# A fused convolution and feed-forward kernel whose start-up is rearranged: first convolution over four quadrants, transposes inside unit 0, second convolution in two cuts

## The chip, the cores and the metric

The kernel runs on one core of a Trainium2 chip. The metric is the device time of one execution in microseconds (us). A profile of one execution gives, for each engine, when every instruction ran: TensorE (PE, with its weight loads as PEld), VectorE (DVE), ScalarE (ACT), GpSimd (POOL) and SyncE (SP). PE multiplies; DVE and ACT copy, scale and add; POOL and SP here mostly start DMA transfers.

## The reference

```python
def _attn_ref(x, weight):              # x (8, 4096, 192) f32, weight (8, 7)
    w = np.exp(weight - np.max(weight, axis=-1, keepdims=True))
    w = w / (np.sum(w, axis=-1, keepdims=True) + 1e-09)
    x_pad = np.concatenate([np.zeros((B, 6, D)), x], axis=1)
    idx = np.arange(S)[:, None] + np.arange(7)[None, :]
    x_unf = x_pad[:, idx, :].reshape(B, S, 7, H, D // H)
    return np.einsum('hk,bskhg->bshg', w, x_unf).reshape(B, S, D)

def _moe_ref(x, w_in, w_out):          # w_in (192, 2048), w_out (2048, 192)
    h = x @ w_in
    return np.maximum(0.01 * h, h) @ w_out
```

A causal convolution with seven taps along the sequence (the taps are a softmax, one set for each of eight heads of 24 channels), and then a two-layer network with a leaky ReLU between the layers, for 32768 tokens.

## The kernel before

The 192 channels are cut into three chunks of 64. The eight sequences are worked on in pairs: one sequence of a pair lies on partitions 0 to 63, the other on 64 to 127 (called `e` = 0 and 1). A block is 512 tokens of both sequences of a pair; there are 32 blocks. The first two blocks are cut in halves of 256 tokens, so the work runs over `groups`: four halves, then 30 whole blocks.

For a group, three things happen. The convolution makes `yt` from `xt` (x, transposed so that channels lie on partitions). `mm1` multiplies `yt` by `w_in` into a PSUM tile `ph` (128 x 1024 f32) and ACT turns `ph` into `g` with the leaky ReLU (L501); for a half group there are eight such units, called U0 to U7 here for the first group, and U8 and on for the second. Each unit of a half group is 12 matmuls of 256 columns: two slices `i` of the hidden layer, three chunks, two sequences, where the two sequences use different halves of PE's rows and run side by side, so a unit is six pairs. Two `ph` buffers take turns. The second layer multiplies `g` by `w_out` into PSUM (L511 for the four half groups, L574 later); its first three pairs run ahead of U8. DVE makes the convolution of the groups behind the second.

The change lies wholly in the start-up, up to the end of the first group. The order of each engine's instructions is the order in which the program issues them (a manual schedule); an engine waits on semaphores in that order. What is done there, with the lines of the profile:

- POOL starts the transfers of `w_in` (L314, in two column halves of 1024, each in two row parts), `x_rows` (L148: 256 tokens for the second group, then for the third) and `w_out` (L346), and later blocks of x (L152, L99).
- PE keeps itself busy with matmuls of ones (`warm`, L358), spreads the taps over the partitions (`select`, L394: the exponentials as a sum of three bf16 parts, hi, mid and a rest), and transposes the first group's x (L179); ACT copies it to `xt` (L199).
- For the convolution on PE, a tap is a 64 x 64 diagonal matrix, one for each of two bf16 parts (p = 0 is hi, 1 is mid), seven taps and three chunks: `diag[c][:, p, k]`. They are made from an identity `ident2` and the taps `whm` (f32): DVE makes five wide products (L413, seven taps at once, or four for chunk 1), ACT ten single ones (L421). A conv matmul (L257) is 64 x 64 with 256 columns and takes one quadrant of PE: row half by `e`, column half by where its result goes. With `cross` the result of one sequence goes to the other's partitions, so that four matmuls, two straight and two crossed, can run side by side. `run` zips the lists of two chunks, so one place of the order is two or four matmuls. The first convolution takes 28 places: seven of two (chunk 0, hi), seven of four (chunk 0, mid, and chunk 2, hi), seven of four (chunk 1, mid, and chunk 2, mid), seven of two (chunk 1, hi).
- The results are scaled by `rsum` (one over the softmax's sum) while ACT (L452) and DVE (L276, L271) copy them from PSUM to `yt`.
- `w_in` is wanted on both partition halves: `spread_down` (L320) and `spread_up` (L323) copy 64 partitions to the other 64 on DVE.
- PE then transposes the second group's x out of `x_rows[1]` (L188, 12 matmuls, `transpose_first(1)`), DVE copies the result to `xt` (L199), and U0 starts.
- The second group's chunk 1 is convolved on DVE (L226, L232); its chunks 0 and 2 on PE in 14 places of four matmuls, in cuts of 6, 5 and 3 places behind U1, U3 and U5 (`CUTS`). Behind U6, PE transposes the third group's x.

Of the kernel before, what the change touches and what calls it, by code (L numbers as in the profile page):

```python
# [10 lines left out]
FP32 = mybir.dt.float32  # L11
BF16 = mybir.dt.bfloat16
# [3 lines left out]
def kernel(  # L16
# [8 lines left out]
    nc = tc.nc  # L25

    B, S, D = x.shape
    H, K = weight.shape
# [7 lines left out]
    CH = 64  # L36
# [7 lines left out]
    NBLK = (B // 2) * NB  # L44
    NHALF = 2
    RUN = 4
    NPEC = 3
    FILL = 48
    VK = 4
    FIRST = (0, 2, 1)  # L50
    SKEW = [(c, k) for k in range(2) for c in range(2)]
    pair = iter([(0, 2), (1, 2), (0, 3), (1, 3), (0, 4), (1, 4), (0, 5)])
    for k in range(K):
        SKEW += [(2, k), next(pair)]
    SKEW += [(1, 5), (0, 6), (1, 6)]
    CUTS = {1: (0, 6), 3: (6, 11), 5: (11, 14)}
    GB = 32
    NR = D // (2 * GB)

# [135 lines left out]
    def evac_first(q, *copies):  # L195
        dst = xt[0][:, :, HALO + q * HT : HALO + (q + 1) * HT]
        dst = dst.rearrange("p c (s k) -> p s c k", s=HS)
        for s, t in enumerate(ptr.pop(q)):
            copies[s](out=dst[:, s], in_=t)  # L199
# [36 lines left out]
                )  # L236
        return jobs

    def pe_conv_jobs(grp, c, parts=(0, 1), cross=False, apart=False):

        blk, t0, T = grp
        accs = [
            psum_o.tile([128, ST], FP32, name=f"acc{i}", tag="po")
            for i in range(2 if apart else 1)
        ]
        jobs = []
        for p in parts:
            for k in range(K):  # L250
                a = BASE + k + blk * ST + t0
                both = []
                for e in range(2):
                    ps = slice(e * CH, (e + 1) * CH)
                    to = slice((e ^ cross) * CH, ((e ^ cross) + 1) * CH)
                    both.append(
                        lambda k=k, p=p, a=a, ps=ps, to=to, acc=accs[e * apart]: nc.tensor.matmul(  # L257
                            out=acc[to, :T], lhsT=diag[c][ps, p, k, :],
                            rhs=xt[0][ps, c, a : a + T],
                            start=(k == 0 and p == parts[0]),  # L260
                            stop=(k == K - 1 and p == parts[1]),
                        )
                    )
                jobs.append(both)

        def evac(*scale):
            if blk not in yt:
                yt[blk] = yt_pool.tile([128, NCH, ST], BF16, name="yt")
            y = yt[blk][:, c, t0 : t0 + T]
            if not cross:  # L270
                scale[0](y, accs[0][:, :T], rsum[:, c, :])  # L271
                return
            for e in range(2):
                ps = slice(e * CH, (e + 1) * CH)
                frm = slice((1 - e) * CH, (2 - e) * CH)
                scale[e](y[ps], accs[e * apart][frm, :T], rsum[frm, c, :])  # L276

        return jobs, evac

    def run(*lists):  # L280
        for slots in zip_longest(*lists, fillvalue=()):
            for both in slots:
                for job in both:
                    job()
# [31 lines left out]
            in_=moe_w_in[rows : rows + ps[1], n * WF : (n + 1) * WF],  # L316
        )

    def spread_down(n):
        nc.vector.tensor_copy(out=w_in[n][0:CH, 1, :], in_=w_in[n][CH:128, 0, :])  # L320

    def spread_up(n):
        nc.vector.tensor_copy(out=w_in[n][CH:128, 1:3, :], in_=w_in[n][0:CH, 0:3:2, :])  # L323

    def w_in_of(f, e, c, m0, m1):
        n, f = divmod(f, NFC // NPW)
# [29 lines left out]
    def warm(n, cols=HT):  # L356
        for _ in range(n):
            nc.tensor.matmul(  # L358
                out=wa[:, 0, 0:cols], lhsT=ones[:, 0:128], rhs=ones[:, 0:cols],
                start=True, stop=True,  # L360
            )
# [41 lines left out]
    cast_first(0, 0, nc.scalar.copy)  # L403
    cast_first(0, 1, nc.scalar.copy, slice(0, 1))
    cast_first(0, 1, nc.vector.tensor_copy, slice(1, 2))
    whm = const_pool.tile([128, NCH, 2, K + 1], FP32, name="whm")
    nc.vector.tensor_copy(out=whm, in_=wps_hm)


    diag = [const_pool.tile([128, 2, K, CH], BF16, name=f"diag{c}") for c in range(NPEC)]  # L410

    def diag_wide(c, p, n):
        nc.vector.tensor_mul(  # L413
            diag[c][:, p, 0:n],
            ident2[:, None, :].to_broadcast([128, n, CH]),
            whm[:, c, p, 0:n, None].to_broadcast([128, n, CH]),
        )

    def diag_each(c, p, ks):
        for k in ks:  # L420
            nc.scalar.activation(  # L421
                out=diag[c][:, p, k, :], in_=ident2,
                func=mybir.ActivationFunctionType.Copy, scale=whm[:, c, p, k : k + 1],
            )


    warm(1, 192)
    transpose_first(0, lambda: select(wps_l, slice(2, 3)))
    wps_l = wps_l[:, :, 0, 0]
    warm(1, ST)  # L430
    warm(1, 384)
    evac_first(0, nc.scalar.copy, nc.scalar.copy)
    for p in range(2):
        diag_wide(0, p, K)
    diag_wide(2, 0, K)
    diag_wide(1, 1, VK)
    diag_wide(2, 1, K)
    diag_each(1, 1, range(VK, K))
    diag_each(1, 0, range(K))
    wml = const_pool.tile([128, NCH, K + 1], FP32, name="wml")  # L440
    nc.vector.tensor_add(wml, wps_l, whm[:, :, 1])
    rsum = const_pool.tile([128, NCH, 1], FP32)
    nc.vector.scalar_tensor_tensor(
        out=rsum, in0=wml[:, :, K:], scalar=1e-9, in1=whm[:, :, 0, K:],
        op0=mybir.AluOpType.add, op1=mybir.AluOpType.add,
    )
    nc.vector.reciprocal(rsum, rsum)
    spread_down(0)
    spread_up(0)

    def act_scale(out, in_, scale):
        nc.scalar.activation(  # L452
            out=out, in_=in_, func=mybir.ActivationFunctionType.Copy, scale=scale
        )

    pe_0, evac_0 = pe_conv_jobs(groups[0], 0)
    pe_2, evac_2 = pe_conv_jobs(groups[0], 2, cross=True, apart=True)
    pe_1, evac_1 = pe_conv_jobs(groups[0], 1, (1, 0))
    run(pe_0[:K])
    run(pe_0[K:], pe_2[:K])  # L460
    evac_0(act_scale)
    run(pe_1[:K], pe_2[K:])
    run(pe_1[K:])
    evac_2(act_scale, nc.vector.tensor_scalar_mul)
    evac_1(act_scale)
    transpose_first(1)
    evac_first(1, nc.vector.tensor_copy, nc.vector.tensor_copy)
    wk = const_pool.tile([128, NCH, K], FP32, name="wk")
    nc.vector.tensor_add(wk, whm[:, :, 0, 0:K], wml[:, :, 0:K])
    nc.vector.tensor_mul(wk, wk, rsum.to_broadcast([128, NCH, K]))  # L470


    g, po, acc2, osb, seal = {}, {}, {}, {}, None
# [8 lines left out]
    def mm1(grp, u, M):  # L482
        blk, t0, T = grp
        y = yt[blk]
        nf = ST // T
        ph = psum_h.tile([128, 2, ST], FP32, name="ph", tag="ph")
        chunks = range(NCH) if blk or t0 else FIRST
        for n in range(nf * NCH):
            i, c = n // NCH, chunks[n % NCH]
            f = nf * u + i  # L490
            for e in range(2):
                ps = slice(e * CH, (e + 1) * CH)
                for m in range(0, 128, M):
                    nc.tensor.matmul(  # L494
                        out=ph[m : m + M, e, i * T : (i + 1) * T],
                        lhsT=w_in_of(f, e, c, m, m + M),
                        rhs=y[ps, c, t0 : t0 + T],
                        start=(c == chunks[0]),
                        stop=(c == chunks[-1]),
                    )  # L500
        act = nc.scalar.activation(  # L501
            out=g[blk][:, nf * u : nf * (u + 1), :, t0 : t0 + T],
            in_=ph.rearrange("p e (i t) -> p i e t", i=nf),
            func=mybir.ActivationFunctionType.Prelu, alpha=0.01,
        )
        return act
# [149 lines left out]
    for i, grp in enumerate(groups):  # L656
# [11 lines left out]
        for j in range(steps):  # L668
            early = between.get((i, j), (0, 0))
            for u in range(2 * j, 2 * j + 2):  # L670
                mm2_slots(i, early[u % 2])
                mm1(grp, u, 128 if i <= NSW else CH)
                if i == 0 and u == 0:
                    conv_1 = conv_jobs(groups[1], (1,))
                    for job in conv_1[:3]:
                        job()
                    spread_down(1)
                    spread_up(1)
                    for job in conv_1[3:]:
                        job()  # L680
                    pe_0, evac_0 = pe_conv_jobs(groups[1], 0)
                    pe_2, evac_2 = pe_conv_jobs(groups[1], 2, cross=True)
                if i == 0 and u in CUTS:
                    cut = slice(*CUTS[u])
                    run(pe_0[cut], pe_2[cut])
                if i == 0 and u == 5:
                    evac_0(nc.vector.tensor_scalar_mul)
                    evac_2(nc.vector.tensor_scalar_mul, nc.vector.tensor_scalar_mul)
                if i == 0 and u == 6:
                    transpose_first(2)  # L690
            jobs = ahead[per * j : per * (j + 1)]
            if T == ST:

# [3 lines left out]
                    job()  # L697
                jobs = []
            mm2_slots(i, quota[j] - sum(early))
            if i == 0 and j == 3:  # L700
                evac_first(2, nc.vector.tensor_copy, nc.vector.tensor_copy)
            if i == 1 and j == 1:
                load_x(3, transpose_x(2))
            for job in jobs:
# [47 lines left out]
```

## Time and profile before

| what | value |
|---|---|
| median of 4 runs | 681.21 us (681.05 to 681.47) |
| the profiled execution | 681.47 us |
| its span (first to last instruction) | 679.7 us |
| first matmul of U0 starts | 9.46 us |
| DVE busy / ACT busy | 481.2 / 518.7 us |
| granted PE clock from 3.5 us on | 1.0 |

The span is what the profile's instructions cover; the rest of the time lies around it. A timeline line has the start in us from the span's beginning, the time that the merged instructions cover, engine, line of the program and operation, tiles written and read, the shape, how many instructions were merged, and in brackets how long the engine was idle before and what released it. A busy engine is not always an engine that does new work: a matmul's record is longer (0.27 us for 256 columns) than the distance to the next one (0.11 us).

### The profile page before, as it was taken

Reading aid. Unit: us, or ns where it says so; the run is one execution under the profiler, and the core shown is the slowest. Engines: PE = TensorE matmul, PEld = TensorE weight load, DVE = VectorE, ACT = ScalarE, POOL = GpSimd, SP = SyncE. Lnnn points to the kernel's source line nnn. Section 1 sums busy time; section 2 is a strip of 40 time slices with the busy share of each in tenths; the row PEclk is TensorE's granted clock in tenths of the full one; section 3 lists DMA queues with packets and bytes.
Section 4 is the critical chain, followed back from the end, with each engine's and each line's share of the span. In section 5 each row is a group of like instructions: output and inputs, shape, how many; then the busy total and the mean of one; then the engine's idle time right before and its main releaser. Section 6 shows DMA issues by size and latency. Waiting matters only on the chain.

```text
span 679.7 us, 27093 instructions
## 1 busy us (share of the span) xinstructions
PE 675.4 (99%) x12444; PEld 446.8 (66%) x12444; DVE 481.2 (71%) x811; ACT 518.7 (76%) x608; POOL 146.7 (22%) x205
## 2 busy tenths in 40 slices
PE   9999999999999999999999999999999999999998
PEld 6997666666666666666666666666666666666667
DVE  7989468766768667778667687667786676876612
ACT  7899777777777778777777877777777777777781
POOL 7455210222201222102222012222022220000000
PEclk9999999999999999999999999999999999999999
DMA  9898846666647557456566476565565573321123
GB/s 153 96 106 111 57 78 89 80 63 74 90 77 96 71 55 89 80 87 87 63 66 92 76 95 76 56 85 83 84 87 67 62 96 72 72 56 33 34 49 94
DMA packets 213890, 53.27 MB, mean 78 GB/s; under 512 B 209296, under 2 KB 213392, under 8 KB 213776
## 3 DMA queue, kind: packets, MB, share of 16 engines
q0 software_dynamic: 98752, 13.97, 30.2%
q1 hardware_dynamic: 115008, 37.57, 27.7%
q8 instruction: 97, 1.59, 1.0%
q14 instruction: 17, 0.14, 0.1%
q10 hardware_dynamic: 16, 0.00, 0.0%
HBM read 28.31 MB, written 25.17 MB: 79 GB/s over the span
## 4 chain that ended last, share of the span: by engine, by line
PE 98%; DMA 1%; POOL 0%; issue 0%; DVE 0%; POOLq 0%
PE ph L494 49%; PE acc L574 44%; PE po L511 5%; DMA x_rows<-in_x_dram 1%; PE acc L257 0%; POOL w_in L314 0%; PE ptr L188 0%; POOL x_rows L148 0%; POOL sel L300 0%; DVE o_sb L624 0%; POOL ident masks.py:199 0%; POOL sel L298 0%; POOL ident masks.py:197 0%; POOLq masks.py:199 0%; POOLq L736 0%
## 5 line engine op out<-in xcount | busy, mean ns | idle before, releaser
L501 ACT ACTIVATE g<-ph 128x1024 bf16<-128x1024 f32 x512 | 496.6, 1021 | 140.7 <-PE ph L494 140.5
L232 DVE SCALAR_TENSOR_TENSOR yt<-xt,wk,yt 128x512 bf16<-128x512 bf16 (+1 forms) x582 | 381.2, 726 | 0.2
L494 PE MATMUL ph<-yt,w_in 64*64 64x512 bf16 (+2 forms) x6048 | 377.1, 369 | 0.0
L574 PE MATMUL acc<-g,w_out 64*64 64x512 bf16 x5568 | 339.9, 376 | 0.0
L494 PEld LDWEIGHTS <-w_in 64*64 64x64 bf16 (+1 forms) x6048 | 229.1, 131 | 103.1 <-issue 0.8
L574 PEld LDWEIGHTS <-w_out 64*64 64x64 bf16 x5568 | 178.6, 118 | 118.7
L99 POOL DMA_DIRECT2D x_bf<-in_x_dram x180 | 134.3, 777 | 410.4 <-DMA xt<-x_bf 408.6
L596 DVE STREAM_TRANSPOSE o_t<-acc 128x512 f32<-128x512 f32 x87 | 73.3, 883 | 181.5 <-PE acc L574 181.5
L511 PE MATMUL po<-w_out,g 64*128 64x192 bf16 (+1 forms) x640 | 36.8, 243 | 0.0
L511 PEld LDWEIGHTS <-g 64*128 64x128 bf16 (+1 forms) x640 | 32.5, 95 | 3.2 <-issue 0.4
L226 DVE TENSOR_SCALAR yt<-xt,wk 128x512 bf16<-128x512 bf16 (+1 forms) x97 | 29.1, 325 | 3.4 <-DMA xt<-x_bf 3.2
L584 ACT COPY junk<-junk 128x1 f32<-128x1 f32 x58 | 11.1, 192 | 4.1
L624 DVE COPY o_sb<-po 128x192 f32<-128x192 f32 x8 | 2.8, 357 | 6.8 <-PE po L511 3.8
L257 PE MATMUL acc<-xt,diag 64*64 64x256 bf16 x140 | 5.5, 272 | 0.2 <-ACT xt L199 0.2
L624 ACT COPY o_sb<-po 128x192 f32<-128x192 f32 x16 | 5.1, 324 | 0.3
L257 PEld LDWEIGHTS <-diag 64*64 64x64 bf16 x140 | 4.3, 106 | 1.3 <-DVE diag L413 0.6
L152 POOL DMA_DIRECT2D x_half<-in_x_dram x6 | 4.3, 726 | 1.1 <-DMA w_in<-in_moe_w_in_dram 0.9
L358 PE MATMUL warm<-const-bfloat16-1.0 128*128 128x512 bf16 (+3 forms) x12 | 3.7, 457 | 0.8 <-PEq L736 0.8
L358 PEld LDWEIGHTS <-const-bfloat16-1.0 128*128 128x128 bf16 x12 | 1.4, 127 | 2.5 <-issue 2.5
L148 POOL DMA_DIRECT2D x_rows<-in_x_dram x4 | 2.9, 741 | 0.0
L413 DVE TENSOR_TENSOR diag<-ident,whm 128x448 bf16<-128x448 bf16 (+1 forms) x5 | 2.6, 581 | 0.0
L421 ACT ACTIVATE diag<-ident,whm 128x64 bf16<-128x64 bf16 x10 | 2.5, 335 | 0.0
(47 smaller groups left out, 23.7 us busy)
## 6 DMA issues: line engine op xcount, KB each, us to landing
out_dram<-o_t SPq DMA_DIRECT2D x112, 192.0 KB, 4.6
x_bf<-in_x_dram POOLq DMA_DIRECT2D x180, 64.0 KB, 3.1
out_dram<-o_sb SPq DMA_DIRECT2D x8, 192.0 KB, 3.0
xt<-x_bf SPq DMA_TRANSPOSE x90, 3.7
w_out<-in_moe_w_out_dram POOLq DMA_DIRECT2D x2, 384.0 KB, 7.8
out_dram<-o_t SPq DMA_DIRECT2D x8, 96.0 KB, 2.3
out_dram<-o_sb SPq DMA_DIRECT2D x8, 96.0 KB, 1.7
w_in<-in_moe_w_in_dram POOLq DMA_DIRECT2D x2, 256.0 KB, 5.1
```

What stands on the lines that cost most here:

```text
L99: ins = nc.gpsimd.dma_start(out=t[:, c, :, e, :], in_=src[2 * rp + e, :, :, c * CH : (c + 1) * CH],)
L226: lambda s=src, d=dst, c=c: nc.vector.tensor_scalar_mul(d, s, wk[:, c, 0:1])
L232: lambda s=src, d=dst, c=c, k=k: nc.vector.scalar_tensor_tensor(out=d, in0=s, scalar=wk[:, c, k : k + 1], in1=d, op0=mybir.AluOpType.mult, ...
L257: lambda k=k, p=p, a=a, ps=ps, to=to, acc=accs[e * apart]: nc.tensor.matmul(out=acc[to, :T], lhsT=diag[c][ps, p, k, :], rhs=xt[0][ps, c, a ...
L358: nc.tensor.matmul(out=wa[:, 0, 0:cols], lhsT=ones[:, 0:128], rhs=ones[:, 0:cols], start=True, stop=True,)
L494: nc.tensor.matmul(out=ph[m : m + M, e, i * T : (i + 1) * T], lhsT=w_in_of(f, e, c, m, m + M), rhs=y[ps, c, t0 : t0 + T], start=(c == chun ...
L501: act = nc.scalar.activation(out=g[blk][:, nf * u : nf * (u + 1), :, t0 : t0 + T], in_=ph.rearrange("p e (i t) -> p i e t", i=nf), func=my ...
L511: return nc.tensor.matmul(out=po[m], lhsT=g[b][ps, fc, e, s * 128 : (s + 1) * 128], rhs=w_out[ps, fc, :], start=start, stop=stop,)
L574: ins = nc.tensor.matmul(out=acc2[gi, r][e * CH : (e + 1) * CH, 0:T], lhsT=w_out_of(ps, fc, r), rhs=g[b][ps, fc, e, t0 : t0 + T], start=fi ...
L584: seal = nc.scalar.copy(out=junk, in_=junk)
L596: nc.vector.transpose(out=osb[gi, 0][:, 0 : T // GB, :, r], in_=acc2.pop((gi, r))[:, 0:T].rearrange("p (j k) -> p j k", k=GB),)
L624: ins = copy(out=o_sb[:, n % 2, :], in_=po.pop(n))
```

## The change

In words, in the order of the program:

- Taps: `whm` (f32) becomes `taps` (bf16), each tap stored twice side by side. All six diagonals (three chunks, two parts) are made by DVE, by a product over pairs of neighbouring columns; ACT makes none.
- One more warm-up matmul of 192 columns stands ahead of the first convolution.
- First convolution in 21 places of four: chunk 0's hi taps go straight into one PSUM tile and its mid taps crossed into another at the same time; then chunks 1 and 2, hi then mid, at the same time. The two tiles of chunk 0 are joined: ACT scales the crossed one into an f32 tile `low`, and DVE computes `hi * rsum + low`. One half of chunk 2 uses a bank of the `wps` tile.
- `spread_up(0)` is split in two copies, one ahead of `spread_down(0)` and one behind the join; `wk` (f32 taps for DVE's convolution) is computed earlier.
- The transposes of `x_rows[1]` move from ahead of U0 to the inside of U0: U0 does chunk 0 for both slices, then the transposes run, then chunks 1 and 2. The DVE copies follow U0 in the program.
- Second convolution: cuts of 7 and 7 places behind U1 and U4, its evacuation behind U4's cut; the third group's transposes behind U5 and not U6, and the DVE copies of them directly after.

```diff
-    CUTS = {1: (0, 6), 3: (6, 11), 5: (11, 14)}
+    CUTS = {1: (0, K), 4: (K, 2 * K)}
...
+    def y_of(grp, c):
         blk, t0, T = grp
...
+        if blk not in yt:
+            yt[blk] = yt_pool.tile([128, NCH, ST], BF16, name="yt")
+        return yt[blk][:, c, t0 : t0 + T]
+
+    def acc_tile():
+        return psum_o.tile([128, ST], FP32, name="acc", tag="po")
...
-        def evac(*scale):
...
+        def evac(*scale, out=None):
+            out = y_of(grp, c) if out is None else out
             if not cross:
-                scale[0](y, accs[0][:, :T], rsum[:, c, :])
+                scale[0](out, accs[0][:, :T], rsum[:, c, :])
                 return
...
+    def spread_up(n, slots=slice(0, 3, 2), copy=nc.vector.tensor_copy):
+        to = slice(slots.start // 2 + 1, (slots.stop - 1) // 2 + 2)
+        copy(out=w_in[n][CH:128, to, :], in_=w_in[n][0:CH, slots, :])
...
-    whm = const_pool.tile([128, NCH, 2, K + 1], FP32, name="whm")
-    nc.vector.tensor_copy(out=whm, in_=wps_hm)
+    taps = const_pool.tile([128, NCH, 2, K + 1, 2], BF16, name="taps")
+    nc.vector.tensor_copy(
+        out=taps, in_=wps_hm[..., None].to_broadcast([128, NCH, 2, K + 1, 2])
+    )
...
+    def diag_wide(c, p):
+        shape = [128, K, CH // 2, 2]
         nc.vector.tensor_mul(
-            diag[c][:, p, 0:n],
-            ident2[:, None, :].to_broadcast([128, n, CH]),
-            whm[:, c, p, 0:n, None].to_broadcast([128, n, CH]),
-        )
+            diag[c][:, p].rearrange("p k (m t) -> p k m t", t=2),
+            ident2.rearrange("p (m t) -> p m t", t=2)[:, None].to_broadcast(shape),
+            taps[:, c, p, 0:K, None, :].to_broadcast(shape),
+        )
...
     warm(1, 384)
+    warm(1, 192)
     evac_first(0, nc.scalar.copy, nc.scalar.copy)
-    for p in range(2):
-        diag_wide(0, p, K)
-    diag_wide(2, 0, K)
-    diag_wide(1, 1, VK)
-    diag_wide(2, 1, K)
-    diag_each(1, 1, range(VK, K))
-    diag_each(1, 0, range(K))
...
+    diag_wide(0, 0)
+    diag_wide(0, 1)
+    diag_wide(1, 0)
+    nc.vector.tensor_add(wml, wps_l, taps[:, :, 1, :, 0])
+    diag_wide(2, 0)
...
+    diag_wide(1, 1)
     nc.vector.reciprocal(rsum, rsum)
+    diag_wide(2, 1)
+    spread_up(0, slice(0, 1))
     spread_down(0)
-    spread_up(0)
+    wk = const_pool.tile([128, NCH, K], FP32, name="wk")
+    nc.vector.tensor_add(wk, taps[:, :, 0, 0:K, 0], wml[:, :, 0:K])
+    nc.vector.tensor_mul(wk, wk, rsum.to_broadcast([128, NCH, K]))
...
-    pe_0, evac_0 = pe_conv_jobs(groups[0], 0)
-    pe_2, evac_2 = pe_conv_jobs(groups[0], 2, cross=True, apart=True)
-    pe_1, evac_1 = pe_conv_jobs(groups[0], 1, (1, 0))
-    run(pe_0[:K])
-    run(pe_0[K:], pe_2[:K])
-    evac_0(act_scale)
-    run(pe_1[:K], pe_2[K:])
-    run(pe_1[K:])
-    evac_2(act_scale, nc.vector.tensor_scalar_mul)
+    hi = acc_tile()
+    low = const_pool.tile([128, HT], FP32, name="low")
+    pe_hi, _ = pe_conv_jobs(groups[0], 0, parts=(0,), accs=[hi] * 2)
+    pe_lo, evac_lo = pe_conv_jobs(groups[0], 0, cross=True, parts=(1,))
+    run(pe_hi, pe_lo)
+    evac_lo(act_scale, act_scale, out=low)
+    nc.vector.scalar_tensor_tensor(
+        out=y_of(groups[0], 0), in0=hi[:, :HT], scalar=rsum[:, 0, :], in1=low,
+        op0=mybir.AluOpType.mult, op1=mybir.AluOpType.add,
+    )
+    spread_up(0, slice(2, 3))
+    pe_1, evac_1 = pe_conv_jobs(groups[0], 1)
+    pe_2, evac_2 = pe_conv_jobs(groups[0], 2, cross=True, accs=[acc_tile(), wps[:, 0]])
+    run(pe_1, pe_2)
     evac_1(act_scale)
-    transpose_first(1)
-    evac_first(1, nc.vector.tensor_copy, nc.vector.tensor_copy)
...
+    evac_2(nc.vector.tensor_scalar_mul, act_scale)
...
+        wide = not (blk or t0 or u)
+        order = [(i, c) for i in range(nf) for c in chunks]
+        if wide:
+            order = [(i, c) for c in chunks for i in range(nf)]
+        for i, c in order:
+            if wide and (i, c) == (0, 1):
+                transpose_first(1)
...
                 if i == 0 and u == 0:
+                    evac_first(1, nc.vector.tensor_copy, nc.vector.tensor_copy)
                     conv_1 = conv_jobs(groups[1], (1,))
-                    for job in conv_1[:3]:
+                    for job in conv_1[:2]:
                         job()
                     spread_down(1)
+                    conv_1[2]()
                     spread_up(1)
...
-                if i == 0 and u == 5:
+                if i == 0 and u == 4:
                     evac_0(nc.vector.tensor_scalar_mul)
                     evac_2(nc.vector.tensor_scalar_mul, nc.vector.tensor_scalar_mul)
-                if i == 0 and u == 6:
+                if i == 0 and u == 5:
                     transpose_first(2)
+                    evac_first(2, nc.vector.tensor_copy, nc.vector.tensor_copy)
...
-            if i == 0 and j == 3:
-                evac_first(2, nc.vector.tensor_copy, nc.vector.tensor_copy)
```

`pe_conv_jobs` now takes its PSUM tiles from its caller if there are any, and only the parts that it is asked for; the rest of the kernel is unchanged.

## The prediction

> **What bounds the kernel now.** I read the page's first part, then the chain that ended last in order of time, then the timeline of TensorE (PE), ScalarE (ACT) and VectorE (DVE) for the first 20 us, where every line of the change runs.
>
> ```profile
> PE 675.4 (99%) x12444; PEld 446.8 (66%) x12444; DVE 481.2 (71%) x811; ACT 518.7 (76%) x608; POOL 146.7 (22%) x205
> ```
> PE is busy 675.4 of 679.7 us. It pays for everything ahead of its steady part, and nothing later gives that back.
>
> ```profile
> 4.31 4.65 DMA x_rows<-in_x_dram
> ...
> 9.00 0.52 PE ptr L188 x11
> 9.52 1.43 PE ph L494 x24
> ```
> The chain runs over a transfer: the second half of x_rows lands at 8.96, eleven transposes start at 9.00, the first layer follows.
>
> ```profile
> 9.46 1.50 PE L494 MATMUL ph<-yt,w_in 64*128 64x256 bf16 x24
> 10.88 0.85 PE L257 MATMUL acc<-xt,diag 64*64 64x256 bf16 x24
> 11.67 1.51 PE L494 MATMUL ph<-yt,w_in 64*128 64x256 bf16 x24
> 13.11 0.74 PE L257 MATMUL acc<-xt,diag 64*64 64x256 bf16 x20
> 13.78 1.61 PE L494 MATMUL ph<-yt,w_in 64*128 64x256 bf16 x24
> 15.33 0.52 PE L257 MATMUL acc<-xt,diag 64*64 64x256 bf16 x12
> 15.78 0.85 PE L494 MATMUL ph<-yt,w_in 64*128 64x256 bf16 x12
> 16.56 0.53 PE L188 MATMUL ptr<-ident,x_rows 128*64 128x128 bf16 x12
> 17.02 0.85 PE L494 MATMUL ph<-yt,w_in 64*128 64x256 bf16 x12
> 17.70 0.41 PE L511 MATMUL po<-w_out,g 64*128 64x192 bf16 x6
> ```
> This is PE's timeline: start, length, instructions. Twelve matmuls of L494 are one unit, so the order is U0 U1, conv, U2 U3, conv, U4 U5, conv, U6, transposes, U7, then three pairs of L511 and U8 at 17.95. I take the prices from starts. Later in the timeline 24 matmuls of L494 that follow L511 take 1.31 us (20.33 to 21.64): 0.109 a pair, 0.655 a unit. U0 and U1 take 1.42 up to the conv, and 24 conv matmuls (six places of four) 0.79 = 6 x 0.11 + 0.13. So each change between L494 and the conv costs about 0.12 us, and a conv place 0.11.
>
> ```profile
> 10.34 1.94 ACT L501 ACTIVATE g<-ph 128x1024 bf16<-128x1024 f32 x2 [1.17 <-PE ph L494]
> 12.56 1.94 ACT L501 ACTIVATE g<-ph 128x1024 bf16<-128x1024 f32 x2 [0.28 <-PE ph L494]
> 14.67 3.02 ACT L501 ACTIVATE g<-ph 128x1024 bf16<-128x1024 f32 x3 [0.17 <-PE ph L494]
> 17.91 2.99 ACT L501 ACTIVATE g<-ph 128x1024 bf16<-128x1024 f32 x3 [0.21 <-PE ph L494]
> ```
> ACT empties each unit's ph in 1.02 us, every 0.92 at best (1.94 for two). A unit fills ph in 0.655. There are two ph buffers, so unit n can't start until ACT has finished unit n-2. The convs between the units give ACT that time. U2 starts at 11.67, its last pair 0.57 later, that ends 0.27 later (12.51), and ACT starts at 12.56: a unit costs 0.89 from its first pair to ACT's start behind a change, 0.86 without.
>
> **The change, part by part.** POOL's and SP's instructions keep their order, so every DMA is issued in the old sequence.
>
> *First conv.* It ran in 28 places from 5.30 to 8.39 and will run in 21. It starts when ACT's second copy of xt ends, as before (the added warm-up matmul of 192 columns, some 0.08 us, falls into the 0.19 that PE waits for that copy), so seven places, 0.77 us, go. None of that is gain by itself: L188 waits for 8.96 in any case. ACT loses ten L421 (2.49 us) and gains one more evacuation (0.47); both lie before 9 us, where ACT was waiting 1.17 us for U0.
>
> *Diagonals.* DVE now makes all six wide products with bf16 taps.
> ```profile
> 3.80 0.17 DVE L383 TENSOR_TENSOR ident<-ident 128x64 bf16<-128x64 bf16 x1
> ...
> 4.41 2.57 DVE L413 TENSOR_TENSOR diag<-ident,whm 128x448 bf16<-128x448 bf16 x5
> ```
> With fp32 taps L413 takes 621 ns for 448 elements and 421 for 256: 1.04 ns an element, 0.154 fixed, and the next starts 0.54 behind. The new form, all bf16, isn't in the trace. L383 is a product of the same type, all bf16: 173 ns for 64 elements, where 0.154 + 64 x 1.04 would be 221, and products of 21 fp32 elements take 174 and 182. So all-bf16 runs faster than one element per 1.04 ns. Upper bound 621 (the pair broadcast does not keep that rate), lower bound 0.154 + 448 x 0.30 = 290 (the slope that L383 gives with that fixed cost). I take half the slope, 0.52, as a fixed cost of 0.14 would make it: 0.39 each, one per 0.30.
>
> Then DVE runs: taps 4.18 to 4.43 (0.20 for L407's 48 elements, 96 now); the six products with the three small rsum steps to 6.63; two w_in spreads at 0.42 (L320; the first half of w_in landed at 6.16, 4.3 us after its issue) to 7.55; wk's two steps to 7.97; the new sum of hi and low, priced as L232's 0.49, 7.88 to 8.37; the last spread to 8.82; chunk 2's half (0.46) to 9.32. PE: chunk 0 conv 5.30 to 6.10, chunks 1 and 2 to 7.63, each product ready before its turn. ACT's two halves of low end at about 7.4, before DVE asks. U0's chunk 0 starts on PE at 8.42, its two pairs are issued by 8.67, and the transposes, after a change, could start at 8.76. They wait for 8.96 as before. The cover is 0.25 us. The two DVE copies behind them follow at 9.56 as before, with wk already done.
>
> [...]
>
> [...]
>
> *Unit 0.* Its two pairs of chunk 0 run ahead of the transposes, so four are left at 9.46 instead of six: **-0.22**.
>
> *Second conv.* 14 places as before, in two cuts and not three: two changes fewer, **-0.24**. Before, U5 waited a little for ACT (24 matmuls took 1.55 from 13.78 to the conv, with one change 1.43): **-0.09** (the rest is rounding).
>
> *What takes it back.* With U2, U3, U4 in a row ACT is late. U1 starts at 9.92, conv 10.67, U2 11.56, U3 12.24, U4 could go at 12.89. ACT starts on U2 at 11.56 + 0.89 = 12.45, ends at 13.47, PE hears of it about 0.05 later: U4 at 13.51, **+0.62**. Queued behind it on PE are U4, the second cut, U5 and everything else; ACT's next unit and DVE's evacuations wait for those. Conv 14.26, U5 15.15, transposes 15.92, U6 16.38; U7 could start at 17.06 and waits for ACT on U5 (16.04 + 1.02 + 0.05 = 17.11): **+0.05**. Before, transposes stood between U6 and U7 and covered ACT; now U6, U7 and three pairs of L511 (0.25) stand before U8, which could go at 18.00 but waits for ACT on U6: 16.38 + 0.89 + 1.02 + 0.05 = 18.34, **+0.34**. From there L511 and L494 alternate, PE needs 2.63 a pair of units against ACT's 2.16 with its copies, and the offset stays.
>
> Sum of the terms: -0.55 + 1.01 = +0.46. Directly, U8 goes from 17.95 to 18.34: +0.39. I take **+0.4**. The moved DVE work (two copies of xt before unit 6, evacuations after U4's cut, ending near 16.8) is done before U8 asks. The profiled execution lasted 681.47, 1.77 around its span of 679.7; it would become 681.9. The median lies 0.26 below it, so I forecast 681.21 + 0.4 = **681.6 us**.
>
> **Rivals.** (1) Slower: the pair broadcast runs at L413's old rate. Place: DVE before U0. Six products at 0.54 and not 0.30 put the sum of hi and low at 9.77; two pairs, a change and the transposes follow, and U0's rest starts near 10.61, not 9.46: +1.15 and the same ACT waits, **682.8**. It decides once a product's step exceeds 0.30 by 0.25/6 = 0.04. For it: the broadcast has no row here. Against: L383. (2) ACT covers the run of three after all and the saving stays: 681.21 - 0.55 = **680.7**. For it: PE shows no wait on ACT in the old profile, against it: U5's late start and the 1.02 of every L501. (3) Nothing happens on the path, since U0 still waits for x_rows, and the small gains and waits cancel: **681.2**. For it, the chain's DMA of 4.65; against, the three waits do not depend on it.
>
> **How the numbers follow.** Forecast 0.60, rival 1 0.13, rival 2 0.17, rival 3 0.08, others 0.02. The range reaches from rival 2 to rival 1: 680.6 to 682.8. A change of 0.2% is 1.36 us, about what can be told from none. Only rival 1 passes it (+1.55, and not all of its ways are that large): slower 0.10. No sum found here reaches -1.36: faster 0.02, same 0.88.
>
> **What would show it.** Right: the six products near 0.39 us; conv ended by 7.9; the sum of hi and low by 8.4; eleven transposes at 9.00; U1 at 9.92; a gap in PE of about 0.6 before U4 with ACT as releaser; U8 at 18.3. Wrong: products of 0.62, U0's rest after 10, no gap before U4, or a transfer that lands at another time than 8.96.

## The result and the profile after

The changed kernel takes 682.04 us in the median (682.0 to 682.87, 33 runs), the kernel before 681.44 (681.04 to 682.19, 53 runs). The ratio is 1.0012 with a 95% interval of 1.0007 to 1.0017: 0.5 to 1.2 us slower. That is less than the 0.2% that the prediction calls about what can be told from none, yet the interval lies clear of 1. The two profiled spans are 680.3 and 679.7 us.

The timeline of PE in the changed kernel, lines as before (L504 is the old L494, L185 the old L188, L260 the old L257, L522 the old L511, L512 the old L501):

```profile
8.69 0.41 PE L504 MATMUL ph<-yt,w_in 64*128 64x256 bf16 x4 [0.71 <-DVE yt L464]
9.03 0.53 PE L185 MATMUL ptr<-ident,x_rows 128*64 128x128 bf16 x12
9.48 1.38 PE L504 MATMUL ph<-yt,w_in 64*128 64x256 bf16 x20
10.80 0.96 PE L260 MATMUL acc<-xt,diag 64*64 64x256 bf16 x28
11.69 1.50 PE L504 MATMUL ph<-yt,w_in 64*128 64x256 bf16 x24
13.66 0.85 PE L504 MATMUL ph<-yt,w_in 64*128 64x256 bf16 x12 [0.46 <-ACT g L512]
14.44 0.96 PE L260 MATMUL acc<-xt,diag 64*64 64x256 bf16 x28
15.33 0.85 PE L504 MATMUL ph<-yt,w_in 64*128 64x256 bf16 x12
16.11 0.53 PE L185 MATMUL ptr<-ident,x_rows 128*64 128x128 bf16 x12
16.57 1.58 PE L504 MATMUL ph<-yt,w_in 64*128 64x256 bf16 x24
17.95 0.45 PE L522 MATMUL po<-w_out,g 64*128 64x192 bf16 x6
18.53 0.85 PE L504 MATMUL ph<-yt,w_in 64*128 64x256 bf16 x12
```

Read it beside the one before. U2 and U3 (11.69) would end their issue at 13.04; U4 starts at 13.66, and the bracket names ACT. (The bracket says 0.46, less than the 0.62 from issue to issue, since the last matmul's record still runs.) Three pairs of L522 from 17.95 take 0.25, so U8 could start at 18.20, and starts at 18.53. Before, U8 started at 17.95. PE's steady part begins 0.58 us later, and the span is 0.6 longer: nothing behind U8 gives it back or adds to it.

The timeline of ACT shows why:

```profile
10.25 1.94 ACT L512 ACTIVATE g<-ph 128x1024 bf16<-128x1024 f32 x2 [1.28 <-PE ph L504]
12.58 2.98 ACT L512 ACTIVATE g<-ph 128x1024 bf16<-128x1024 f32 x3 [0.40 <-PE ph L504]
16.22 1.02 ACT L512 ACTIVATE g<-ph 128x1024 bf16<-128x1024 f32 x1 [0.65 <-PE ph L504]
17.46 4.05 ACT L512 ACTIVATE g<-ph 128x1024 bf16<-128x1024 f32 x4 [0.21 <-PE ph L504]
```

ACT starts on U2 at 12.58 and is done 1.02 later, at 13.60; U4 needs that buffer. U6 begins 17.46 on ACT, ends at 18.48, and U8 follows at 18.53. ACT itself stands idle ahead of U2 (0.40) and ahead of U5 (0.65): the two engines wait for each other in turn.

VectorE ahead of U0 (L325 and L321 are the old L323 and L320, the spreads of w_in; L438 sums the small parts of the taps, from which rsum and wk are made):

```profile
5.43 0.18 DVE L438 TENSOR_TENSOR wml<-warm,taps 128x24 f32<-128x24 f32 x1
...
6.74 0.42 DVE L325 COPY w_in<-w_in 64x1024 bf16<-64x1024 bf16 x1
7.18 0.64 DVE L321 COPY w_in<-w_in 64x1024 bf16<-64x1024 bf16 x1
7.83 0.18 DVE L450 TENSOR_TENSOR wk<-taps,wml 128x21 f32<-128x21 bf16 x1
8.05 0.18 DVE L451 TENSOR_TENSOR wk<-wk,rsum 128x21 f32<-128x21 f32 x1
8.15 0.48 DVE L464 SCALAR_TENSOR_TENSOR yt<-acc,rsum,low 128x256 bf16<-128x256 f32 x1
8.66 0.56 DVE L325 COPY w_in<-w_in 64x1024 bf16<-64x1024 bf16 x1
9.26 0.49 DVE L277 TENSOR_SCALAR yt<-acc,rsum 64x256 bf16<-64x256 f32 x1
```

The join of hi and low (L464) ends at 8.63 and not at 8.37: the second spread took 0.64, not 0.42, and ended at 7.82 where the forecast had 7.55. The third took 0.56. The chain that ended last no longer holds a transfer of x_rows:

```profile
1.86 4.86 DMA w_in<-in_moe_w_in_dram
...
7.18 0.64 DVE w_in L321
...
8.15 0.49 DVE yt L464
```

The first part of w_in lands at 6.72 (6.16 before), the spreads and the join follow. The landing itself costs little: VectorE's last product ends at 6.65. Chunk 2's half (L277) ends at 9.75, so U0 waits once more, and U1 starts at 10.02. The transposes stand at 9.03, near the forecast's 9.00, but by luck: x_rows landed at about 8.9 (4.6 us after its issue at 4.3), and they follow U0's first pairs, which waited for the join.

### The profile page after: what moved, and what is told of

It reads as the page before. It is cut to its first block, busy times and chain, and to the rows that moved or that the text cites. A ratio compares the mean times of both kernels' runs of the same rounds, so it can differ in the third digit from the quotient of the medians.

```text
span 680.3 us, 27088 instructions
## 1 busy us (share of the span) xinstructions
PE 675.0 (99%) x12445; PEld 448.1 (66%) x12445; DVE 481.5 (71%) x814; ACT 516.9 (76%) x599; POOL 147.3 (22%) x205
## 4 chain that ended last, share of the span: by engine, by line
PE 98%; DMA 1%; DVE 0%; ACT 0%; POOL 0%; issue 0%; POOLq 0%
PE ph L504 49%; PE acc L585 44%; PE po L522 5%; DMA w_in<-in_moe_w_in_dram 1%; ACT g L512 0%; PE acc L260 0%; PE ptr L185 0%; POOL sel L301 0%; DVE w_in L321 0%; DVE yt L464 0%; DVE w_in L325 0%; DVE o_sb L635 0%; POOL sel L299 0%; DVE wk L450 0%; DVE wk L451 0%
## 5 line engine op out<-in xcount | busy, mean ns | idle before, releaser
L512 ACT ACTIVATE g<-ph 128x1024 bf16<-128x1024 f32 x512 | 496.7, 1021 | 141.1 <-PE ph L504 140.8
L504 PE MATMUL ph<-yt,w_in 64*64 64x512 bf16 (+2 forms) x6048 | 378.3, 369 | 1.3 <-DVE yt L464 0.7
L504 PEld LDWEIGHTS <-w_in 64*64 64x64 bf16 (+1 forms) x6048 | 231.0, 131 | 104.0 <-issue 1.6
L522 PE MATMUL po<-w_out,g 64*128 64x192 bf16 (+1 forms) x640 | 37.7, 243 | 0.0
L522 PEld LDWEIGHTS <-g 64*128 64x128 bf16 (+1 forms) x640 | 34.1, 95 | 2.3 <-issue 0.4
L260 PE MATMUL acc<-xt,diag 64*64 64x256 bf16 x126 | 4.4, 271 | 0.2 <-ACT xt L196 0.2
L260 PEld LDWEIGHTS <-diag 64*64 64x64 bf16 x140 | 3.7, 106 | 0.8 <-issue 0.4
L315 POOL DMA_DIRECT2D w_in<-in_moe_w_in_dram x4 | 2.4, 596 | 0.0
```

The source lines that it names most:

```text
L260: lambda k=k, p=p, a=a, ps=ps, to=to, acc=accs[e]: nc.tensor.matmul(out=acc[to, :T], lhsT=diag[c][ps, p, k, :], rhs=xt[0][ps, c, a : a + T ...
L504: nc.tensor.matmul(out=ph[m : m + M, e, i * T : (i + 1) * T], lhsT=w_in_of(f, e, c, m, m + M), rhs=y[ps, c, t0 : t0 + T], start=(c == chun ...
L512: act = nc.scalar.activation(out=g[blk][:, nf * u : nf * (u + 1), :, t0 : t0 + T], in_=ph.rearrange("p e (i t) -> p i e t", i=nf), func=my ...
L522: return nc.tensor.matmul(out=po[m], lhsT=g[b][ps, fc, e, s * 128 : (s + 1) * 128], rhs=w_out[ps, fc, :], start=start, stop=stop,)
```

## The experiments

The theory is the forecast's: ScalarE is late in the run U2 U3 U4, and again at U8. The rival: the time is lost ahead of U0, in VectorE's longer queue. The kernels ran in three groups (the first four, the next four, the last three), each together with the kernel before on one chip; the third group's chip is another than that of the first two.

**The second convolution put back.** The three old cuts, the evacuation behind U5 and the third group's transposes with their copies behind U6.

```diff
-    CUTS = {1: (0, K), 4: (K, 2 * K)}
+    CUTS = {1: (0, 6), 3: (6, 11), 5: (11, 14)}
...
-                if i == 0 and u == 4:
+                if i == 0 and u == 5:
...
-                if i == 0 and u == 5:
+                if i == 0 and u == 6:
```

> The changed kernel with the second convolution put back: cuts of 6, 5 and 3 places behind U1, U3 and U5, its evacuation behind U5, the third group's transposes behind U6. Theory (ScalarE is late in the run U2 U3 U4 and in U6 U7 U8): the waits of 0.62 and 0.32 us go, 0.24 us of changes come back; U8 starts near 17.9 us instead of 18.53, and the time is 0.5 to 0.7 us under the changed kernel, within 0.2 us of the kernel before. Rival (the time is lost ahead of U0, by VectorE's spreads and the late join of hi and low): nothing is gained, U8 stays near 18.5.

Measured 681.47 us in the median (681.31 to 682.06, 11 runs), before 681.43; ratio 1.0003 (0.9995 to 1.0012). Seven executions lie at 681.31 to 681.48, four at 682.02 to 682.06: a lower and an upper heap. The changed kernel has two as well, near 682.02 and 682.72 (more on them below), so both heaps are 0.7 us lower here. The profile is one of the four, so its start is later throughout, but its units read:

```profile
12.29 1.50 PE L504 MATMUL ph<-yt,w_in 64*128 64x256 bf16 x24
13.72 0.74 PE L260 MATMUL acc<-xt,diag 64*64 64x256 bf16 x20
14.40 1.62 PE L504 MATMUL ph<-yt,w_in 64*128 64x256 bf16 x24
```

No gap follows U3, and U8 starts 6.28 us behind U2 (18.57). In the changed kernel it is 6.84 (11.69 to 18.53), in the kernel before 6.28 (11.67 to 17.95). The theory holds; the rival's "nothing gained" falls. U8's expected 17.9 was not seen, since the profile came from the upper heap.

**The second convolution's new places alone**, in the kernel before: evacuation behind U4, the transposes and their copies behind U5.

```diff
-    CUTS = {1: (0, 6), 3: (6, 11), 5: (11, 14)}
+    CUTS = {1: (0, K), 4: (K, 2 * K)}
...
-                if i == 0 and u == 5:
+                if i == 0 and u == 4:
...
-                if i == 0 and u == 6:
+                if i == 0 and u == 5:
                     transpose_first(2)
+                    evac_first(2, nc.vector.tensor_copy, nc.vector.tensor_copy)
...
-            if i == 0 and j == 3:
-                evac_first(2, nc.vector.tensor_copy, nc.vector.tensor_copy)
```

> The kernel before with the second convolution's new places alone: cuts of 7 and 7 behind U1 and U4, evacuation behind U4, transposes behind U5. Theory: a gap of about 0.62 us before U4 and 0.3 before U8, U8 near 18.6 instead of 17.95, 0.6 to 0.7 us slower than the kernel before. Rival (the loss lies ahead of U0): two changes of shape fewer, 0.2 us faster or no difference.

Measured 682.23 (681.85 to 682.82, 11 runs); ratio 1.0012 (1.0004 to 1.0021), that is 0.8 us over the kernel before. Its timeline has the same gap without any of the start-up's change:

```profile
12.08 1.50 PE L494 MATMUL ph<-yt,w_in 64*128 64x256 bf16 x24
14.04 0.85 PE L494 MATMUL ph<-yt,w_in 64*128 64x256 bf16 x12 [0.46 <-ACT g L501]
```

U8 follows U2 by 6.83 us (18.91), as in the changed kernel; it is later than the expected 18.6 because U0 started at 9.75 in this execution. So the second convolution's places make the loss by themselves.

**Two cuts, but behind U1 and U3**, with the evacuation behind U3.

```diff
-    CUTS = {1: (0, K), 4: (K, 2 * K)}
+    CUTS = {1: (0, K), 3: (K, 2 * K)}
...
-                if i == 0 and u == 4:
+                if i == 0 and u == 3:
```

> The changed kernel with its two cuts of seven behind U1 and U3 instead of U1 and U4, the rest as changed. Theory: no run of three units, so the gap before U4 goes; small waits for ScalarE of 0.1 to 0.25 us before U6, U7 and U8 take part of it back: U8 near 18.0, 0.5 us under the changed kernel. Rival (the loss lies ahead of U0): U8 stays near 18.5.

Measured 681.73 (681.41 to 682.16, 11 runs); ratio 1.0005 (0.9997 to 1.0014). Its U4 starts at 14.01 right behind the cut, U8 at 17.93 as expected, 6.24 us behind U2. That is hardly better than the 6.28 of the three old cuts: U6 and U7 take 1.57 us here (15.97 to 17.54) and 1.38 in the changed kernel, so waits take most of the two saved changes back, as expected. Two cuts cost nothing; the run of U2, U3 and U4 does.

**The changed kernel again.**

> The changed kernel itself once more, as the measure for the other three on the same chip: 0.6 us slower than the kernel before by both theories.

Measured 682.62 (682.01 to 682.74, 11 runs); ratio 1.0015 (1.0006 to 1.0024). That is 1.2 us over the kernel before by medians, not the expected 0.6. The median differs from the first 682.04 because the executions fall into two heaps, near 682.02 and 682.72, in changing shares. This time the profile came from the upper heap. The same stretch of PE's timeline, first in the profile of the lower heap, then of the upper:

```profile
4.63 0.63 PE L360 MATMUL warm<-const-bfloat16-1.0 128*128 128x512 bf16 x3
5.47 1.07 PE L260 MATMUL acc<-xt,diag 64*64 64x256 bf16 x31 [0.21 <-ACT xt L196]
```

```profile
4.75 1.11 PE L360 MATMUL warm<-const-bfloat16-1.0 128*128 128x512 bf16 x3
5.79 1.47 PE L260 MATMUL acc<-xt,diag 64*64 64x256 bf16 x31
...
9.39 0.41 PE L504 MATMUL ph<-yt,w_in 64*128 64x256 bf16 x4 [0.70 <-DVE yt L464]
```

The trace records the full PE clock from 4.47 us in the first and from 6.65 in the second. Ahead of that moment matmuls go at half the speed: in the first profile the next warm-up follows one of 512 columns by 0.43 us at 1.22 and at 1.65, and by 0.22 at 4.63. With the late rise the three warm-up matmuls take 1.11 us and not 0.63, the conv stands behind them and no longer waits for ACT, and its first 31 matmuls take 1.20 us up to the next one's start (5.79 to 6.99), not 0.81 (5.47 to 6.28). U0 starts at 9.39, not 8.69: the 0.70 between the heaps. But the conv is not what U0 waits for: ACT has both halves of low at 8.18, and the join starts at 8.85. The join waits for its turn on VectorE, whose queue is late from L438 on:

```profile
5.90 0.18 DVE L438 TENSOR_TENSOR wml<-warm,taps 128x24 f32<-128x24 f32 x1 [0.42 <-PE warm L360]
...
7.15 0.67 DVE L325 COPY w_in<-w_in 64x1024 bf16<-64x1024 bf16 x1
7.83 0.69 DVE L321 COPY w_in<-w_in 64x1024 bf16<-64x1024 bf16 x1
```

This step reads the tile `warm`, which the warm-up matmuls write too, so it waits for the last of them: 5.90 and not 5.43. The first spread starts 0.41 later than in the lower heap, and the second ends 0.70 later (8.52, not 7.82). The eleven profiles with the changed start-up show such jumps: the second spread ends at 7.81 or 7.82 in the eight whose first spread starts between 6.60 and 6.96, at 8.52 or 8.53 in the two where it starts at 7.15 and 7.47, and at 9.22 in the one where it starts at 8.13 (plain taps, below). So in these profiles a small delay ahead of the spreads costs nothing or a whole 0.70 us.

The clock isn't the only source of such a delay. In the profile of the first experiment, from its upper heap, the clock rose at 6.09, but the chain that ended last also runs over the transfer of the first tokens (x_nat): it landed at 4.28, and VectorE casts it from 4.30 on, in the changed kernel from 3.96.

**wk later.** VectorE's two steps for wk moved from ahead of the join to behind the copies of the second group's x, in the first experiment's kernel.

```diff
-    nc.vector.tensor_add(wk, taps[:, :, 0, 0:K, 0], wml[:, :, 0:K])
-    nc.vector.tensor_mul(wk, wk, rsum.to_broadcast([128, NCH, K]))
...
                     evac_first(1, nc.vector.tensor_copy, nc.vector.tensor_copy)
+                    nc.vector.tensor_add(wk, taps[:, :, 0, 0:K, 0], wml[:, :, 0:K])
+                    nc.vector.tensor_mul(wk, wk, rsum.to_broadcast([128, NCH, K]))
```

> The first experiment's kernel (second convolution in its old places) with VectorE's two steps for wk moved from ahead of the join of hi and low to behind the copies of the second group's x. Theory (with the changed start-up, VectorE's queue ahead of the join decides when U0 starts): the join starts about 0.35 us earlier, U0's chunk 0 near 8.35 in an execution whose clock rises early, the transposes again start when x_rows lands (8.7 to 8.9), and the time falls by 0.1 to 0.25 us against the first experiment (681.32 in most of its executions). Rival (U0 waits for x_rows alone, as forecast): no difference.

Measured 681.14 (680.92 to 681.72, 11 runs), before 681.3 in this group; ratio 0.9999 (0.999 to 1.0008). The lower heap falls from 681.32 to 680.93, 0.4 us, more than expected; the upper from 682.03 to 681.65. The profiled execution, 681.14, is of neither heap. Its timeline of PE shows U0 at 8.39 and the transposes stretched over a wait:

```profile
8.39 0.41 PE L502 MATMUL ph<-yt,w_in 64*128 64x256 bf16 x4 [0.30 <-DVE yt L462]
8.73 0.73 PE L185 MATMUL ptr<-ident,x_rows 128*64 128x128 bf16 x12
9.39 1.28 PE L502 MATMUL ph<-yt,w_in 64*128 64x256 bf16 x20
```

Twelve transposes cover 0.73 us here and 0.53 in the changed kernel. The page names no releaser; x_rows landed at about 8.9 (4.6 us after its issue at 4.3) and the second transpose starts at 8.93, so it is x_rows that they wait for again. In the lower heap, 0.2 us faster, there is likely no such wait: in a profile of 680.97 (this kernel with fewer warm-ups, below) the transposes cover 0.55. So 0.36 us of wk on VectorE did lie on the path ahead of U0; of the rival this part is true.

**Two chunks of U0 ahead of the transposes**, added to that.

```diff
-            if wide and (i, c) == (0, 1):
+            if wide and (i, c) == (0, 2):
                 transpose_first(1)
```

> As the run above, and two chunks of U0, not one, ahead of the transposes. Theory: two more pairs, 0.22 us, leave the stretch behind x_rows; 0.1 to 0.2 us under the run above, near 681.0, which would be 0.3 us under the kernel before's median. Rival (the queue of VectorE is so late that the pairs only push the transposes back): no difference or slower.

Measured 681.62 (680.93 to 682.23, 11 runs); ratio 1.0001 (0.9992 to 1.001). The lower heap is the same 680.93, so the expected 0.2 us did not come; the median is higher because six of 11 executions fell into the upper heap. The expectation was wrong. The profile, from the lower heap, shows what its floor is: U0 starts at 8.39 as in the run above, PE waits for no transfer from there to U8 (17.46), and the join starts at 7.85, right behind the second spread, which ends at 7.81. With PE never waiting for x_rows, moving pairs ahead of the transposes has nothing to gain.

**Plain taps.** The products read one bf16 tap with a step of 0.

```diff
-            diag[c][:, p].rearrange("p k (m t) -> p k m t", t=2),
-            ident2.rearrange("p (m t) -> p m t", t=2)[:, None].to_broadcast(shape),
-            taps[:, c, p, 0:K, None, :].to_broadcast(shape),
+            diag[c][:, p],
+            ident2[:, None, :].to_broadcast([128, K, CH]),
+            taps[:, c, p, 0:K, 0, None].to_broadcast([128, K, CH]),
```

> The changed kernel with its diagonal products read from one bf16 tap with a step of 0, not from pairs. Theory of the forecast's first rival (without the pairs the product runs at one element per 1.04 ns): 0.62 us a product, the last one 1.3 us later, U0's start later by as much, about 683.3 us, 1.3 above the changed kernel. Rival (any all-bf16 product runs at the fast rate): 0.39 us and no difference.

Measured 683.44 (683.41 to 683.47, 6 runs); ratio 1.003 (1.0018 to 1.0043), 1.4 us over the changed kernel's lower heap. VectorE's groups of this line, first in the changed kernel, then here:

```profile
L420 DVE TENSOR_TENSOR diag<-ident,taps 128x448 bf16<-128x448 bf16 x6 | 2.1, 383 | 0.0
```

```profile
L420 DVE TENSOR_TENSOR diag<-ident,taps 128x448 bf16<-128x448 bf16 x6 | 3.5, 614 | 0.0
```

Same type, same size: 383 ns with pairs, 614 without. All-bf16 is not enough, so the theory holds.

**The transposes ahead of U0.**

```diff
+    transpose_first(1)
...
-            if wide and (i, c) == (0, 1):
-                transpose_first(1)
```

> The changed kernel with the transposes of x_rows back ahead of U0. Theory (U0 waits for VectorE's join, so the transposes find PE idle in either place): within 0.15 us of the changed kernel. Rival (the move into U0 earns its 0.22 us): 0.2 us slower than the changed kernel.

Measured 682.03 (682.01 to 682.72, 11 runs), with the changed kernel's two heaps. U0 starts at 8.69 and U1 at 10.02, both as in the changed kernel. The move into U0 earned nothing here, because chunk 2's half, the last of VectorE's steps for U0, ends at 9.75 in both:

```profile
9.80 1.07 PE L503 MATMUL ph<-yt,w_in 64*128 64x256 bf16 x16 [0.48 <-DVE yt L277]
```

PE had idle time for the transposes in either place.

**Fewer warm-up matmuls**, in three kernels: two chunks first, wk later, and the changed kernel.

```diff
     warm(1, ST)
-    warm(1, 384)
-    warm(1, 192)
     evac_first(0, nc.scalar.copy, nc.scalar.copy)
```

> The kernel with two chunks of U0 ahead of the transposes, without the warm-up matmuls of 384 and 192 columns ahead of the first convolution. The executions of the changed kernel fall into two heaps, 682.02 and 682.72, and two of its profiles show the clock rising at 4.47 and at 6.65 us. Theory (with a late clock the two warm-ups take 0.62 us at half speed and hold the first convolution behind them to 5.79, 0.3 us after ACT's copy): the upper heap falls from 681.65 to about 681.35, the lower one stays at 680.93. Rival (the warm-ups hold the clock up; without them it rises later): both heaps stay or rise.

> The same omission in the kernel with wk moved later and one chunk ahead of the transposes. Theory: upper heap from 681.65 to about 681.35, lower heap unchanged at 680.92, median at or under 681.1. Rival: both heaps stay or rise.

> The same omission in the changed kernel. Theory: upper heap from 682.72 to about 682.4, lower heap unchanged at 682.02. Rival: both heaps stay or rise.

Measured 681.04 (680.92 to 681.67), 680.94 (680.92 to 681.33) and 682.03 (682.01 to 682.77), 11 runs each, before 681.4; ratios 0.9995 (0.9986 to 1.0004), 0.9994 (0.9985 to 1.0003) and 1.0009 (1.0 to 1.0018). The lower heaps stay, as expected. The upper heaps did not simply move by 0.3 us: they nearly vanish. In the changed kernel ten of 11 executions lie at 682.01 to 682.04, one at 682.77; the first kernel has one at 681.67, the second none above 681.33, where two lie (the theory had put the heap there). The theory had the wrong path, the conv. In these three profiles VectorE's step for wml no longer waits for PE and starts at 5.39 to 5.42, the first spread at 6.64 to 6.67, and the second ends at 7.81 or 7.82. So the queue can be some 0.3 us later than there before the second spread jumps by 0.70. This is argued from the traces and not fully shown: when the clock rises varies by itself (4.47 and 6.65 in two profiles of the changed kernel), no profile without these warm-ups recorded a rise later than 5.46, and in this group, on its chip, no kernel with the changed start-up ran with them. Nothing speaks for the rival: in the profiles of the second and third the clock rises at 5.46, within the range of the others (3.55 to 6.65); but two records don't refute it. The second is the fastest version found, with a median 0.5 us under the kernel before, but its interval holds 1.

## Why the prediction was right, and where it was off

*ScalarE's waits.* Forecast 0.62 before U4, 0.05 before U7, 0.34 before U8; the profile has 0.62, 0.04 and 0.33. The old places take them away, the new places alone bring them, and a cut behind U3 avoids the first. This is shown. From U1's start to U8's the changed kernel takes 8.51 us and the kernel before 7.81 (10.14 to 17.95). The forecast's terms come near these 0.70 us: the three waits, 0.99, less the two gains of 0.24 and 0.09, make 0.66.

*Two changes fewer, -0.24.* Each of the four changes that are left costs what was read (28 conv matmuls, seven places, take 0.89 = 7 x 0.11 + 0.12). With two cuts behind U1 and U3 most of the gain went into new waits, so no run shows it in the time by itself.

*Diagonals.* 0.39 forecast, 366 to 392 ns measured. There is some luck in it: the slope of 0.52, half of L413's 1.04, was the author's estimate and no row of before showed it; with the fixed cost of 0.14 that goes with it, it would have made 0.37, but 0.154 was added. In the changed kernel the product of 64 elements (L385) took 174 ns and those of 448 took 383, 0.54 ns an element. The first rival's price, 1.15, was 1.4 when its mechanism was built into the changed kernel: the cover of 0.25 that it had to use up first was already gone there, and the second spread's end jumped twice by 0.70 (9.22, not 7.82).

*First conv.* 21 places took 2.24 us from the first matmul's start to the last one's (5.47 to 7.71), 0.11 a step, also in the first seven, where both halves of PE's rows write the tile `hi`. The old second convolution, where both halves write one tile as well, took the same 0.11 a place (0.79 = 6 x 0.11 + 0.13). That it starts as before was wrong by 0.17: 5.47, not 5.30. The clock rose at 4.47, not at 3.55, and three of PE's transposes ahead of ACT's copy took 0.50 us, not 0.34.

*Unit 0, -0.22.* This is the mis-sized term. The cover of 0.25 us ahead of the transposes counted each spread of w_in at 0.42 us. The second took 0.64 and ended 0.27 late (7.82, not 7.55), the third took 0.56, the join ended at 8.63 and chunk 2's half at 9.75, not 9.32, so U1 came at 10.02, not 9.92: -0.12. The landing of w_in, 0.56 later than before, is not the cause: in the changed kernel without the two warm-ups the first spread starts at 6.64, straight behind the last product, and the join still at 8.15. That 0.10 and small steps of 0.01 to 0.03 at the changes carry U8 to 18.53 where 18.34 was forecast. The wk experiment shows the tightness of that queue: 0.36 us less in it gave 0.4 in the time.

*What the sum left out.* The clock. The forecast took one moment of its rise. The heaps, 0.70 us apart, put 10 of the first 33 executions at 682.5 or above. The warm-up matmul of 192 columns that was costed at nothing was covered by PE's wait for ACT (0.21 us of it are left at the rise of 4.47) only while the clock was up; with the late clock VectorE waited for the warm-ups, which the forecast did not count as a wait at all.

Forecast +0.4 us on a median of 681.21; measured +0.6 by medians, +0.8 by the ratio. The mechanism was right, its size too small by the two last points. The base was off as well: 681.21 is a median of four executions, 53 gave 681.44, so the forecast of 681.6 falls 0.4 short of 682.04. Rivals 2 and 3 fall with the waits that were seen.

## What to carry to other kernels

Work that stands between the steps of a producer (PE here) is also time that its consumer (ACT) gets to catch up. Before gathering such work into fewer cuts, write the two engines' starts in one table, with the number of buffers between them, and look for the longest run without it. A start-up chain that has just been shortened hands over to the next queue, so a cover of a quarter of a microsecond worked out from one length of one copy is no cover. Warm-up work that a wait hides at full clock (0.63 us here) can be on the path when the clock rises late (1.11 us), and not only on its own engine: look for who waits for the tile that it writes.

## What the runs showed of the hardware

- The recorded full PE clock began at 3.55 us in the profile of the kernel before and at 4.47 and 6.65 in two of the changed kernel, and between 3.55 and 6.65 in twelve profiles, all of programs whose warm-up matmuls start at 0.84 us. This spread of 3.1 us was not put into the forecast, and no run here shows what sets the moment. The recorded stretch at full clock lasted 675.84 us in the profiles of the kernel before and of the changed kernel's lower heap.
- The same copy of 64 x 1024 bf16 took 0.42 to 0.44 us in many places (0.42 in the kernel before) and 0.51 to 0.69 in others (0.64 and 0.56 in the changed kernel, 0.67, 0.69 and 0.56 in its upper heap), in kernels with the same order of instructions. In the start-up the lengthened ones end at few places, 0.70 us apart (7.82, 8.52, 9.22), and GpSimd's instructions that start DMAs follow each other at about the same distance (7.50, 8.21, 8.90 in the changed kernel, 0.71 and 0.69 apart). No run here isolates what lengthens the copy.
